# A transformer layer on one core: six lead-in tiles transposed by DMA, V in whole matmuls, and W1, W2 and Wo read from DRAM blocks

## The chip, the core and the metric

The kernel runs on one core of a Trainium2 chip. It has a matrix engine (PE, or TensorE), whose weight loads the profile lists apart as PEld; a vector engine (DVE); a scalar engine (ACT), which does the exponentials; a small general engine (POOL); and SP, which here issues every DMA. The engines run on their own and wait for each other through semaphores. The metric is the device time of one execution in microseconds; lower is better. A figure of a profile comes from one profiled execution.

## What is computed

One pre-norm transformer layer on 2048 tokens of width 1024, with 32 heads of 32 columns, a full softmax, and a feed-forward part of width 3584 with GELU:

```python
qkv = layernorm(x) @ wqkv                      # 2048 x 3072
p = softmax(q @ k.T * 32 ** -0.5)              # for each head
h = x + (p @ v) @ wo
out = h + gelu(layernorm(h) @ w1 + b1) @ w2 + b2
```

Inputs and output are bfloat16.

## The kernel before

The program is written as a list of tasks. Each task has an engine, an estimated cost, the buffers it reads and writes, and a priority. `Graph.schedule` plays the list through with these estimates and fixes the order of every engine's instructions; `assign` then works out the semaphore waits, and `emit` writes each engine's stream. Each engine does its stream strictly in order. On PE `pick_pe` chooses among the tasks that are ready: scores first (`qk`), then the products of probabilities with V (`pv`) with their row sums (`den`) when enough rounds wait, then the rest (`bg`: projections, Wo, FFN), the earliest in the list first. `merge_tiles` turns long runs of narrow matmuls (four of 32 columns side by side, L546) into whole ones of 128 columns (L549). Whole ones that were asked for as such are at L552, or at L549 after merging.

*Attention.* The 32 heads go in 8 groups of four (128 columns), and the queries in 8 blocks of 256. A job is one query block and one head group. It has 8 rounds, each over 256 keys: `Att.qk` makes the scores of four heads in four PSUM banks (L784), and two exponentials of 1024 columns (L795) write a probability tile (PT, or PX where the tile lies over memory that is used for something else later). `Job.pv` multiplies with V (L821), VectorE adds pairs of probability columns (L836), and `Job.den` sums them on PE (L850). `Job.finish` divides (L866 to L881). PSUM banks 6 and 7 are the only ones for everything else: an accumulating job holds one until it ends, and each background matmul group takes one until it is copied out.

*Lead-in.* For 16 tiles of 128 tokens the kernel loads x (`x_tile`), normalizes it (`layer_norm`, result in `xb`), and transposes it on PE (`tr_tile`: eight transposes into a bank, L619, and one copy out by ACT for tiles 0 to 3 or VectorE for the rest, L628) into `xnT`, which has four chunks of 512 tokens. After every pair of tiles comes half a chunk of keys for head group 0 (`proj_half`, L758), and three jobs (`NLJ`) start on the keys that are there: 24 rounds, whose probabilities wait in 24 tiles. V of head group 0 is made by `proj_v1` in four parts of four tiles, narrow matmuls, copied at L740. The PV of the lead may start when the last of these copies, `gate`, is done (`ready_rounds`), and the pair sums of the lead after `hold`, the last copy of keys. Then `rest_of_projections(g)` makes, for one head group after another, Q of the first 512 tokens, four chunks of keys (`proj`, L669) and V (`proj_v1` for group 1, `proj_v` from group 2, L721). The Q of tokens 512 to 1023 of some groups (`EXTRA` and group 0) goes through a staging buffer of two (`stg`) and a DRAM scratch (`qd`). Three chunks of xnT are put into DRAM scratch too (`xd`), for the Q projections of later query blocks (`late_q`), which run beside the FFN. The weights of the next head groups are loaded (`rest_w`) when the last tile of x has come.

*FFN.* For each block u of 256 tokens: `wo(u)` (its weights in four blocks of 256 columns), `ln2(u)` (layer norm, with the transposes of its two tiles by DMA, L941), `ffn1(u)` (14 blocks of W1 of 256 columns; VectorE adds the bias, and the GELU is built from a Tanh and VectorE steps), and `ffn2(u, j)` (two halves, each of 7 blocks of W2). These run beside the attention of later query blocks. The weights don't stay on chip: every u loads them again, through rings of four W1 slots (which Wo and the late Q use too) and seven W2 slots. All come straight from the inputs, so that one partition's row of a load lies in DRAM in runs of 512 bytes (Wo and W1: 256 columns) or 1024 bytes (W2: 512 columns).

*DMA.* There is one queue, SP's, and it issues in the order that the schedule fixed; an issue that has to wait holds those behind it.

Of the kernel before, what the change touches and what calls it, by code (L numbers as in the profile page):

```python
# [328 lines left out]
def build_kernel(nc, A_x, A_wqkv, A_wo, B_w1, B_b1, B_w2, B_b2, out):  # L329
# [154 lines left out]
    R1 = Rings((ffn, 4), (ffn, 7), ffn, 2)  # L484
    lq, B_lq = sb(xq_lo, "lq", [P, 2, 512], BF, 2)
# [15 lines left out]
    B_xd = [gr.buf() for _ in range(3)]  # L501
    B_qd = [[gr.buf() for _ in range(NCH)] for _ in range(G)]
# [35 lines left out]

    def mm(bank, lhsT, rhs, start, stop, reads, narrow, cols=(0, 512), after=()):

# [221 lines left out]
    class Att:  # L762
# [8 lines left out]
        def qk(self, job, r, s=None):  # L771


            qb, g = job
# [111 lines left out]
    def attention_round(job, r, lag=1):  # L886
        s = att.qk((job.qb, job.g), r)
        pending.append((job, r, s))
        attention_drain(lag)
# [7 lines left out]
    def wblock(R, src_ap, prio=1):  # L897
        s = R.next("w1", R.nw1)
        dma(R.w1[:, s, :, :], src_ap.rearrange("(dc p) c -> p dc c", p=P), P * DC * 512, writes=[R.B_w1[s]], prio=prio)
        return s  # L900

    def wo(u, tail=False):
# [3 lines left out]
        ws = [wblock(R, A_wo[:, 256 * k:256 * k + 256]) for k in range(4)]  # L906
        assert ws == [0, 1, 2, 3]
        for t in range(2):
# [3 lines left out]
            for j in range(2):  # L912
                s = ws[2 * j]
# [73 lines left out]
    def ffn2(u, j, wide=False, W=None, banks=None):  # L987
# [39 lines left out]
    LEAD_ACT = (0, 1, 2, 3)  # L1027
    NLJ = 3
    last_x = []

    def lead_norm(hc):
# [14 lines left out]
    lead_rounds = []  # L1046
    lead_norm(0)
    for hc in range(8):
# [3 lines left out]
        proj_half(1, hc, slot(), ev)  # L1052
        if hc < 7:
            lead_norm(hc + 1)
        for k, r in [(k, hc) for k in range(min(hc, NLJ))] + ([(hc, r) for r in range(hc + 1)] if hc < NLJ else []):
            n = 8 * k + r
            s = NR + 15 if n == 0 else n - 1 if n < 9 else n
            lead_rounds.append((k, r, att.qk((k, 0), r, s)))
    att.rounds = 8
    hold = [t for t in gr.tasks if t.eng == E.DVE][-1:]  # L1060
    for c in range(4):
        proj_v1(4 * c, 0, 4, slot(), "dve", 0, True)
    gate = gr.tasks[-1]
    for k in range(NLJ):
        job = Job(k, 0, slot(2))
        for _, r, s in [x for x in lead_rounds if x[0] == k]:
            job.pv(r, s)
    pool_banks = {6: [t for t in gr.tasks if t.kind == "warm"][-1:], 7: []}
    lx = last_x[-1:]

    def rest_w(blk, c0, c1):
        load_w(blk, -3, c0, c1, after=lx)
# [3 lines left out]
    rest_w(WV, P, 4 * P)  # L1076
    rest_w(WK, 2 * P, 3 * P)
# [36 lines left out]
    EXTRA = [1, 2]  # L1114
    for g in range(1, G):
# [41 lines left out]
    def ready_rounds(now):  # L1157
# [6 lines left out]
        if gate.done is None or gate.done > now + 1e-9:  # L1164
            return 0
# [112 lines left out]
```

## Time and profile before

| | |
|---|---|
| median of 3 runs | 1090.35 us (1087.95 to 1093.55) |
| the profiled execution | 1091.97 us, span 1090.2 us, mean granted PE clock 0.994 |
| HBM read, written | 161.16 MB, 10.49 MB |
| DMA queue of the kernel | 279,968 packets, 175.35 MB, 54.1% of 16 engines' span |
| instruction fetch of the largest stream | 150 packets, 2.46 MB, 0.9% |
| median issue to landing, 512 KB | W1 4.4 us, W2 5.7 us, Wo 4.2 us |

Times in a profile are microseconds from the start of the span, unless a column says ns. A group of instructions is one line, engine and operation with its tiles (out <- in, partitions x elements), its count, busy time and mean duration, and the idle time of the engine just before its members with what ended it. A wait that ends with "issue" is time in which the engine waited for nothing that the profile shows. A window gives, for a stretch, the busy time of PE, PEld, DVE, ACT and POOL with their counts, then the granted clock of PE, the mean busy share of the 16 DMA engines, and GB/s. [...]

### The profile page before, as it was taken

The page shows a single profiled execution, that of the slowest core. Times are in us where ns is not written, and L with a number is a line of the kernel's source. Part 1 is how long each engine was busy: PE and PEld are TensorE (multiplying, and loading weights), DVE is VectorE, ACT ScalarE, POOL GpSimd, SP SyncE. Part 2 cuts the span into 40 slices and gives each one's busy share as a digit, 9 for nine tenths or more (in the row PEclk, how much of TensorE's full clock was granted, in tenths as well). Part 3 has the DMA queues.
Part 4 walks back from the last instruction along what each step waited for, and adds up shares of the span by engine and source line. Part 5 has one row for each costly group of instructions (what it writes and reads, how often), then busy time and mean ns, then how long its engine had stood idle before and what let it go on. Part 6 is the DMA issues. An engine that isn't in the chain of part 4 may idle for free.

```text
span 1090.2 us, 41817 instructions
## 1 busy us (share of the span) xinstructions
PE 1045.6 (96%) x19048; PEld 609.6 (56%) x19107; DVE 755.9 (69%) x1453; ACT 1014.5 (93%) x1116; POOL 43.4 (4%) x110
## 2 busy tenths in 40 slices
PE   8989999998899999999999999999999999999998
PEld 6656555554344664574475457446545754474483
DVE  7886666666576896599489659948974967696401
ACT  4989999999999999999999999999999999999650
POOL 3200000000010001001000100100010000000100
PEclk9999999999999999999999999999999999899999
DMA  7640010008464667665685766567586656987370
GB/s 194 199 123 11 14 41 3 2 3 287 142 167 133 183 180 209 210 189 154 209 251 157 220 215 189 155 217 233 142 239 205 182 179 160 308 236 228 96 246 20
DMA packets 280146, 178.03 MB, mean 163 GB/s; under 512 B 42656, under 2 KB 274976, under 8 KB 279200
## 3 DMA queue, kind: packets, MB, share of 16 engines
q1 hardware_dynamic: 279968, 175.35, 54.1%
q8 instruction: 150, 2.46, 0.9%
q14 instruction: 28, 0.23, 0.1%
HBM read 161.16 MB, written 10.49 MB: 157 GB/s over the span
## 4 chain that ended last, share of the span: by engine, by line
PE 54%; ACT 39%; DVE 5%; issue 1%; DMA 1%; SPq 0%; POOL 0%; POOLq 0%; DVEq 0%
ACT PT L795 35%; PE ps L549 18%; PE ps L546 12%; PE ps L784 8%; PE ps L821 6%; PE ps L552 5%; PE ps L850 3%; ACT PX L795 2%; DVE PS L836 2%; ACT uu L983 2%; DMA xrb<-in_A_x_dram 0%; DVE OD L866 0%; PE ps L1025 0%; SPq L570 0%; DVE OD L873 0%
## 5 line engine op out<-in xcount | busy, mean ns | idle before, releaser
L795 ACT ACTIVATE PT<-ps 128x1024 bf16<-128x1024 f32 x992 | 922.4, 1082 | 14.7 <-PE ps L784 14.3
L836 DVE TENSOR_TENSOR PS<-PT 128x1024 bf16<-128x1024 bf16 x434 | 286.6, 685 | 128.9 <-PE ps L850 68.1
L784 PE MATMUL ps<-QT,KT 32*128 32x256 bf16 x4096 | 205.3, 274 | 10.7 <-ACT PT L795 5.4
L821 PE MATMUL ps<-PT,V 128*32 128x256 bf16 x3968 | 174.4, 274 | 2.8 <-ACT PT L795 2.8
L784 PEld LDWEIGHTS ps<-QT,KT 32*128 32x128 bf16 x4096 | 61.2, 92 | 166.3 <-ACT PT L795 134.8
L850 PE MATMUL ps<-PS,ones 128*32 128x256 bf16 x1792 | 124.6, 275 | 4.8 <-DVE PS L836 4.0
L821 PEld LDWEIGHTS ps<-PT,V 128*32 128x32 bf16 x3968 | 102.1, 97 | 29.4 <-issue 6.8
L549 PE MATMUL ps<-hnT,a_w1r 128*128 128x256 bf16 x949 | 116.5, 274 | 1.1 <-DVE gT L961 0.5
L549 PEld LDWEIGHTS ps<-hnT,a_w1r 128*128 128x128 bf16 x949 | 87.9, 98 | 25.8 <-issue 14.5
L546 PE MATMUL ps<-a_w2r,gT 128*32 128x512 bf16 x1372 | 98.3, 381 | 0.4 <-DVE hch L1007 0.2
L549 PE MATMUL ps<-a_w2r,gT 128*128 128x512 bf16 x382 | 93.8, 380 | 4.2 <-issue 2.9
L546 PE MATMUL ps<-hnT,a_w1r 128*32 128x256 bf16 x2476 | 88.9, 274 | 4.0 <-issue 1.6
L961 DVE TENSOR_TENSOR gT<-ps,b1f 128x512 bf16<-128x512 f32 x98 | 67.2, 686 | 17.5 <-PE ps L546 9.3
L546 PEld LDWEIGHTS ps<-hnT,a_w1r 128*32 128x32 bf16 x2476 | 60.4, 96 | 20.6 <-issue 16.8
L1007 DVE SCALAR_TENSOR_TENSOR hch<-ps,hch 128x512 bf16<-128x512 f32 x32 | 21.9, 685 | 69.9 <-PE ps L552 47.1
L850 PEld LDWEIGHTS ps<-PS,ones 128*32 128x32 bf16 x1792 | 47.0, 96 | 30.7 <-DVE PS L836 14.2
L549 PEld LDWEIGHTS ps<-a_w2r,gT 128*128 128x128 bf16 x413 | 35.2, 98 | 47.4 <-issue 13.4
L549 PE MATMUL ps<-xnT,Wall 128*128 128x512 bf16 (+1 forms) x256 | 53.5, 344 | 4.5 <-DVE rr L876 2.8
L983 ACT ACTIVATE uu<-uu 128x1024 bf16<-128x1024 bf16 x49 | 53.9, 1108 | 0.0
L546 PEld LDWEIGHTS ps<-a_w2r,gT 128*32 128x32 bf16 x1372 | 30.0, 96 | 25.6 <-issue 14.0
L603 POOL CAST mvb<-mv 128x2 bf16<-128x2 f32 (+1 forms) x25 | 4.9, 201 | 987.2 <-DVE mv L600 987.2
L549 PE MATMUL ps<-Wall,xnT 128*128 128x128 bf16 (+1 forms) x443 | 43.9, 247 | 0.0
(89 smaller groups left out, 1007.9 us busy)
## 6 DMA issues: line engine op xcount, KB each, us to landing
a_w2r<-in_B_w_dram SPq DMA_DIRECT2D x105, 512.0 KB, 5.7
a_w1r<-in_B_w_dram SPq DMA_DIRECT2D x98, 512.0 KB, 4.4
a_w1r<-in_A_wo_dram SPq DMA_DIRECT2D x32, 512.0 KB, 4.2
b_w1r<-in_B_w_dram SPq DMA_DIRECT2D x14, 512.0 KB, 6.1
a_w1r<-in_A_wqkv_dram SPq DMA_DIRECT2D x11, 512.0 KB, 5.0
Wall<-in_A_wqkv_dram SPq DMA_DIRECT2D x17, 256.0 KB, 4.7
xrb<-in_A_x_dram SPq DMA_DIRECT2D x16, 256.0 KB, 4.0
hch<-in_A_x_dram SPq DMA_DIRECT2D x16, 256.0 KB, 5.2
```

What stands on the lines that cost most here:

```text
L546: fns.append(lambda p, j=j: p.matmul(psum[32 * j:32 * j + 32, bi(bank), c0:c1], lhsT[:, 32 * j:32 * j + 32], rhs, start=start, stop=stop, ...
L549: t.whole = lambda p: p.matmul(psum[:, bi(bank), c0:c1], lhsT, rhs, start=start, stop=stop, skip_group_check=True)
L552: t = pe(lambda p: p.matmul(psum[:, bi(bank), c0:c1], lhsT, rhs, start=start, stop=stop), occ, reads=reads, writes=[bb(bank)], mode="full" ...
L603: pool(lambda g: g.tensor_copy(mvb[:, sl, :], mv_l[:, sl, :]), 0.25, reads=B_mv[sl], writes=B_mvb[sl], prio=prio)
L784: return p.matmul(psum[:, 2 * us[h // 2] + h % 2, 256 * i:256 * i + 256], KT[32 * h:32 * h + 32, g, k0:k0 + P], QT[32 * h:32 * h + 32, qs, :],
L795: act(lambda a, u=u, k=k: a.activation(PTs[s][:, k, :, :], psum[:, 2 * u:2 * u + 2, :], ACT.Exp, bias=0.0, scale=SCALE), 1024, reads=[B_ps ...
L821: fns.append(lambda p, i=i, h=h: p.matmul(psum[32 * h:32 * h + 32, bi(bank), 0:256], V[:, g, 2 * r + i, 32 * h:32 * h + 32], PTs[s][:, h / ...
L836: dve(lambda v: v.tensor_tensor(PS[:, n, :, :], pairs[:, :, 0:256], pairs[:, :, 256:512], ALU.add), c_dve(1024, 2), reads=B_PTs[s], writes ...
L850: fns.append(lambda p, h=h, rhs=rhs, i=i: p.matmul(psum[32 * h:32 * h + 32, bi(bank), 256:512], ones32[:, :], rhs, start=False, stop=last, ...
L961: t = dve(lambda v: v.tensor_tensor(g[:, fc:fc + 2, :], psum[:, bi(bank), :].rearrange("p (f c) -> p f c", f=2), b1f[:, fc:fc + 2].unsquee ...
L983: act(lambda a: a.activation(w, w, ACT.Tanh, bias=0.0, scale=KT2), 1024, reads=[B_uu[i]], writes=[B_uu[i]], prio=-1)
L1007: drop(dve(lambda v, hs=hs, bank=bank, half=half: v.scalar_tensor_tensor(hch[:, hs, c], psum[:, bi(bank), :], half, hch[:, hs, c], ALU.mul ...
```

## The change

In the lead-in:

- Tiles 10 to 15 are not transposed on PE. A DMA transpose of each normalized tile writes xnT (`LEAD_PE = 10`).
- `proj_v1` is asked for as whole matmuls for head groups 0 and 1.
- `gate` becomes two tasks, the last copy of keys and the last copy of V of the lead, and through `late` every matmul group that the list names after the keys of group 1 waits for both.
- A Q projection that goes through the staging buffer starts only when the buffer is free (`free`).
- The first three `rest_w` loads (group 1's keys and queries, and the rest of V's first block) wait for tile 11 of x instead of tile 15; the others wait for the last DMA transpose. The scratch copies of xnT are issued between them.

For the weights:

- `block_copies` copies Wo (2 blocks of 1 MB), W1 (14 of 512 KB) and W2 (14 of 512 KB) from the inputs into DRAM blocks by 30 DMAs from DRAM to DRAM, in which one partition's row is one run of 4 KB (W1, W2) or 8 KB (Wo). Copy i waits for exponential 96 + 5i.
- All loads of these weights then read the blocks. Wo comes as two tiles of 512 columns (`wov`), each over two W1 slots, instead of four of 256.

```diff
+    wov = [nc.alloc_sbuf_tensor_at("wov%d" % j, [P, DC, 512], BF, offset=R1.B_w1[2 * j].lo) for j in range(2)]
+    w1d = nc.dram_tensor("w1_blocks", [FC // 2, P, DC, 256], BF, kind="Internal").ap()
+    w2d = nc.dram_tensor("w2_blocks", [2, FC // 4, P, 4, 512], BF, kind="Internal").ap()
+    wod = nc.dram_tensor("wo_blocks", [2, P, DC, 512], BF, kind="Internal").ap()
...
     def mm(bank, lhsT, rhs, start, stop, reads, narrow, cols=(0, 512), after=()):
+        after = list(after) + (late if start else [])
...
+        o = B_stg[cnt["sg"] % NSG]
+        free = o.w + o.r if which == 0 and not direct else []
         for dc in range(DC):
             mm(bank, Wall[blk][:, dc, c:c + P], xnT[:, tc, dc, :], dc == 0, dc == DC - 1,
-               [B_W[blk][c // P]] + B_xnTt[tc], True)
+               [B_W[blk][c // P]] + B_xnTt[tc], True, after=free if dc == 0 else ())
...
+    def block_copies():
+
+        jobs = []
+        for j in range(2):
+            jobs.append((wod[j], A_wo[:, 512 * j:512 * j + 512].rearrange("(dc p) c -> p dc c", p=P), P * DC * 1024, B_wod[j]))
+        for k in range(FC // 2):
+            jobs.append((w1d[k], B_w1[:, 256 * k:256 * k + 256].rearrange("(dc p) c -> p dc c", p=P), P * DC * 512, B_w1d[k]))
+        for j in range(2):
+            for q in range(FC // 4):
+                jobs.append((w2d[j, q], B_w2[512 * q:512 * q + 512, 512 * j:512 * j + 512].rearrange("(f p) c -> p f c", p=P),
+                             P * 4096, B_w2d[j][q]))
+        exps = [t for t in gr.tasks if t.kind == "exp"]
+        for i, (o_ap, i_ap, n, b) in enumerate(jobs):
+            dma(o_ap, i_ap, n, writes=[b], prio=3, after=[exps[COPY0 + COPY_STEP * i]])
...
-        ws = [wblock(R, A_wo[:, 256 * k:256 * k + 256]) for k in range(4)]
-        assert ws == [0, 1, 2, 3]
+        for j in range(2):
+            dma(wov[j][:, :, :], wod[j], P * DC * 1024, reads=[B_wod[j]], writes=R.B_w1[2 * j:2 * j + 2], prio=1)
+        R.cnt["w1"] += 4
...
-                    mm(bank, OT[:, u % 3, g, t * P:(t + 1) * P], R.w1[:, s:s + 2, g, :], k == 0, k == 7 and not tail,
+                    mm(bank, OT[:, u % 3, g, t * P:(t + 1) * P], wov[j][:, g, :], k == 0, k == 7 and not tail,
...
-            s = wblock(R, B_w1[:, 256 * blk:256 * blk + 256])
+            s = wblock(R, None, block=blk)
...
-            dma(W.w2[:, s, :, :], B_w2[512 * q:512 * q + 512, c].rearrange("(f p) c -> p f c", p=P),
-                P * 4096, writes=[W.B_w2[s]], prio=1)
+            dma(W.w2[:, s, :, :], w2d[j, q], P * 4096, reads=[B_w2d[j][q]], writes=[W.B_w2[s]], prio=1)
...
+    LEAD_PE = 10
...
-            tr_tile(tt, slot(), "act" if tt in LEAD_ACT else "dve")
+            if tt < LEAD_PE:
+                tr_tile(tt, slot(), "act" if tt in LEAD_ACT else "dve")
+            else:
+                tc, t4 = divmod(tt, 4)
+                last_t[:] = [dma_transpose(xnT[:, tc, :, t4 * P:(t4 + 1) * P], xb[:, tt % NXB, :], P * 2048, [B_xb[tt % NXB]], [B_xnTt[tc][t4]], -4)]
...
-        if hc in (3, 5, 7):
-            tc = hc // 2
-            dma(xd[tc - 1], xnT[:, tc, :, :], P * 8192, reads=B_xnTt[tc], writes=[B_xd[tc - 1]], prio=1)
...
+        lead_k = gr.tasks[-1]
...
-        proj_v1(4 * c, 0, 4, slot(), "dve", 0, True)
-    gate = gr.tasks[-1]
+        proj_v1(4 * c, 0, 4, slot(), "dve")
+    gate = [lead_k, gr.tasks[-1]]
...
-    lx = last_x[-1:]
+    lx = last_x[3:4]
...
     rest_w(WV, P, 4 * P)
+    lx = last_t or last_x[-1:]
+    for tc in range(1, 4):
+        dma(xd[tc - 1], xnT[:, tc, :, :], P * 8192, reads=B_xnTt[tc], writes=[B_xd[tc - 1]], prio=1)
...
             proj(1, g, tc, slot(), "dve")
+        late[:] = gate
         if g == 1:
             for c in range(4):
-                proj_v1(4 * c, 1, 4, slot(), "dve", 0, True, [gate])
+                proj_v1(4 * c, 1, 4, slot(), "dve")
...
+    COPY0, COPY_STEP = 96, 5
...
+    block_copies()
     late_q(1, 1, [g for g in range(2, G) if g not in EXTRA])
```

More of the change, by code (lines that the diff above doesn't have):

```diff
@@ L501, in build_kernel @@
     B_xd = [gr.buf() for _ in range(3)]
+    w1d = nc.dram_tensor("w1_blocks", [FC // 2, P, DC, 256], BF, kind="Internal").ap()
+    w2d = nc.dram_tensor("w2_blocks", [2, FC // 4, P, 4, 512], BF, kind="Internal").ap()
+    wod = nc.dram_tensor("wo_blocks", [2, P, DC, 512], BF, kind="Internal").ap()
+    B_w1d = [gr.buf() for _ in range(FC // 2)]
+    B_w2d = [[gr.buf() for _ in range(FC // 4)] for _ in range(2)]
+    B_wod = [gr.buf() for _ in range(2)]
     B_qd = [[gr.buf() for _ in range(NCH)] for _ in range(G)]
@@ L537, in drop @@
             t.rel = bank
+    late = []
     def mm(bank, lhsT, rhs, start, stop, reads, narrow, cols=(0, 512), after=()):
+        after = list(after) + (late if start else [])
         c0, c1 = cols
@@ L771, in qk @@
         def qk(self, job, r, s=None):
-            qb, g = job
+            qb, g = job.qb, job.g
             qs = q_slots[qb, g]
@@ L886, in attention_round @@
     def attention_round(job, r, lag=1):
-        s = att.qk((job.qb, job.g), r)
+        s = att.qk(job, r)
         pending.append((job, r, s))
@@ L894, in attention_drain, with wblock @@
             job.pv(r, s)
-    def wblock(R, src_ap, prio=1):
+    def block_copies():
[11 more added lines that the diff above has]
+            dma(o_ap, i_ap, n, writes=[b], prio=3, after=[exps[COPY0 + COPY_STEP * i]])
+    def wblock(R, src_ap, prio=1, block=None):
         s = R.next("w1", R.nw1)
+        if block is not None:
+            dma(R.w1[:, s, :, :], w1d[block], P * DC * 512, reads=[B_w1d[block]], writes=[R.B_w1[s]], prio=prio)
+            return s
         dma(R.w1[:, s, :, :], src_ap.rearrange("(dc p) c -> p dc c", p=P), P * DC * 512, writes=[R.B_w1[s]], prio=prio)
@@ L1163, in ready_rounds @@
         waiting = 0
-        if gate.done is None or gate.done > now + 1e-9:
+        if any(x.done is None or x.done > now + 1e-9 for x in gate):
             return 0
```

11 lines of the change are left out of this document (6 added, 5 removed).

## The prediction

> **What bounds the kernel now.** I read the shares of the page first, then what ScalarE waited for, then the stages where it waited.
>
> ```profile
> span 1090.2 us, 41817 instructions
> PE 1045.6 (96%) x19048; PEld 609.6 (56%) x19107; DVE 755.9 (69%) x1453; ACT 1014.5 (93%) x1116; POOL 43.4 (4%) x110
> ACT PT L795 <- PE ps L784: 14.3, 12, 3.8
> 100.00:250.00 150.00, 148.32 (x2944) 87.08 (x2946) 95.65 (x176) 150.00 (x165) 0.00 (x0) 1.00 0.04 12
> 300.00:1000.00 700.00, 679.83 (x13007) 392.26 (x13039) 532.91 (x1023) 693.97 (x754) 22.23 (x56) 1.00 0.67 197
> 1000.00:1020.00 20.00, 18.68 (x373) 9.06 (x372) 9.30 (x17) 20.00 (x23) 0.00 (x0) 1.00 0.62 203
> 1060.00:1075.00 15.00, 14.89 (x83) 8.00 (x83) 0.73 (x2) 2.26 (x5) 0.00 (x0) 1.00 0.03 9
> ```
>
> The windows give start and end, length, then busy time of PE, PEld, DVE, ACT and POOL, granted clock, DMA share and GB/s. ScalarE is busy 150 of 150 us and 693.97 of 700: the exponentials are one unbroken line from 22.91 us to about 1020, and PE (148.32 and 679.83) runs just below it. After 1020 PE alone works, at 14.89 of 15 us, on work the change leaves alone. So time can be won where ScalarE stands still between its third exponential and the last, 14.3 us in twelve waits, and one of these (2.99 us, at 22.91) lies ahead of everything that changes. Here are the others that matter:
>
> ```profile
> 22.91 3.77 ACT L795 ACTIVATE PT<-ps 128x1024 bf16<-128x1024 f32 x4 [2.99 <-PE ps L784]
> 76.51 197.17 ACT L795 ACTIVATE PT<-ps 128x1024 bf16<-128x1024 f32 x214 [3.80 <-PE ps L784]
> 276.83 15.01 ACT L795 ACTIVATE PT<-ps 128x1024 bf16<-128x1024 f32 x16 [1.03 <-PE ps L784]
> ACT PT L795 <- PE ps L784: 8.4, 5, 3.8
> ACT PT L795 <- PE ps L784: 5.8, 7, 1.5
> ```
>
> The last two rows are the same wait within 22 to 300 us (8.4) and within 300 to 1020 (5.8). Taking off 2.99 and 3.80, 1.6 us is left, 1.03 of it at 276.83. Three terms, then: 3.8 in the lead-in, 1.6 at the start of the FFN, 5.8 under the weight traffic.
>
> **The lead-in.** One exponential takes 197.17 / 214 = 0.921 us. The lead has 24 rounds, 48 exponentials; the third starts at 22.91, so they end at 22.91 + 46 x 0.921 = 65.3. Head group 1 follows: rounds 0 to 3 read its first two key chunks (8 exponentials, to 72.7), round 4 the third chunk. ScalarE stops at 76.51 - 3.80 = 72.7 exactly. The third chunk was late:
>
> ```profile
> 55.37 0.68 DVE L740 CAST V<-ps 128x512 bf16<-128x512 f32 x1
> 61.29 0.68 DVE L669 CAST KT<-ps 128x512 bf16<-128x512 f32 x1
> 63.70 6.67 DVE L836 TENSOR_TENSOR PS<-PX 128x1024 bf16<-128x1024 bf16 x11
> 72.09 0.44 DVE L866 STREAM_TRANSPOSE OD<-ps 128x256 f32<-128x256 f32 x1
> 73.13 3.00 PE L549 MATMUL ps<-xnT,Wall 128*128 128x512 bf16 x13 [2.19 <-DVE rr L876]
> 75.11 0.65 DVE L669 CAST KT<-ps 128x512 bf16<-128x512 f32 x1
> ```
>
> Chunk two was copied at 61.29; then the lead's PV jobs held both background PSUM banks while VectorE worked off 11 pair sums, until 72.09, and chunks three and four were multiplied at 73.13. VectorE is the resource: the change takes six of its copies and 48 transposes out ahead of this.
>
> ```profile
> L628 DVE COPY xnT<-ps 128x1024 bf16<-128x1024 bf16 x6 | 4.1, 690 | 1.2 <-PE ps L619 1.1
> L619 PE MATMUL ps<-ident,xb 128*128 128x128 bf16 x48 | 3.7, 219 | 0.2 <-DVE KT L758 0.2
> hnT<-a_xb SPq DMA_TRANSPOSE x14, 3.7
> 313.11 1.24 SPq L575 DMA_TRANSPOSE hnT<-a_xb  x1
> 35.53 0.99 DVE L613 TENSOR_SCALAR xb<-xrb,mvr,rden 128x1024 bf16<-128x1024 bf16 x2
> 48.59 0.99 DVE L613 TENSOR_SCALAR xb<-xrb,mvr,rden 128x1024 bf16<-128x1024 bf16 x2
> 53.09 0.42 DVE L758 CAST KT<-ps 128x256 bf16<-128x256 f32 x1 [1.57 <-PE ps L549]
> ```
>
> So 4.1 us of VectorE and 3.7 of PE's modelled time leave the stretch from 36 to 54 us. In their place stand six DMA transposes: 1.24 us of SP's queue each (7.4 together) and 3.7 from issue to landing. Tiles 10 and 11 are normalized by 36.5 (35.53 + 0.99) and would land near 36.5 + 1.2 + 3.7 = 41.4; their half chunk of keys, the sixth, is wanted after 15 rounds, at 22.91 + 28 x 0.921 = 48.7. The last pair is normalized by 49.6, earlier if VectorE gains; it lands near 54.5 at worst, its keys are ready some 2 us later (eight matmuls and a copy of 0.42), and they are wanted at 22.91 + 40 x 0.921 = 59.8. The cover is about 3 us. SP issues head group 2's weights behind the transposes and the scratch copies of xnT later than before, but neither is read in this stretch. The weights of head group 1 now wait for tile 11 instead of tile 15, so its three later key chunks can be multiplied while the PE has no transposes to do, before PV takes the banks. One chunk ahead of the banks is enough: chunk four is wanted at 22.91 + 58 x 0.921 = 76.3, and the banks came free at 73.13. I take the whole wait, -3.8; bounds 0 (banks still held) and -4.5 (PE ahead as well).
>
> V as whole matmuls and the new waits cost nothing that I can see:
>
> ```profile
> 78.04 1.57 PE L549 MATMUL ps<-Wall,xnT 128*128 128x128 bf16 x25
> 83.59 1.52 PE L546 MATMUL ps<-Wall,xnT 128*32 128x128 bf16 x96
> ```
>
> 25 whole matmuls take 1.57 us, 96 narrow ones (24 whole) 1.52, the same; most of V already ran whole. If whole ones break up narrow runs, a 0.2 us turn on PE comes some eight times: bound +1.6, hidden as long as PE is ahead. The wait on the staging buffer sits only on three Q projections; it frees a bank instead of holding it: 0, bounds -0.5 to +0.5.
>
> **The copies.** Thirty DRAM copies start behind exponentials 96, 101 to 241: by 0.921 us, near 76.5 + 40 x 0.921 = 113 us to 247. There the DMA share is 0.04. They move 16.8 MB each way. No row shows a DRAM-to-DRAM copy; the nearest is a load in 512 B runs (next fence, 286 GB/s): 0.5 MB in 1.8 us, every 4.6 us, a share of 0.4, or 0.8 if reading and writing add up. On SP they are issued behind ScalarE's count, so a load of queries queued behind one can wait up to 4.6 us; these go out a job (16 exponentials, 14.7 us) ahead. What is exposed is PE's instruction supply, below. I take +0.6, bounds 0 and +3.
>
> **The weights in long runs.** These rows show what run length does to a full DMA: 8 KB runs (xq), 512 B (W1), 1 KB (W2).
>
> ```profile
> 262.00:264.00 2.00, 2.00 (x48) 0.92 (x48) 1.27 (x4) 2.00 (x3) 0.00 (x0) 1.00 1.02 431
> 744.50:745.50 1.00, 1.00 (x40) 0.63 (x28) 1.00 (x3) 1.00 (x2) 0.00 (x0) 1.00 0.99 286
> 808.00:811.00 3.00, 3.00 (x37) 1.10 (x39) 0.00 (x0) 3.00 (x5) 0.00 (x0) 1.00 0.93 302
> q8 instruction: 150, 2.46, 0.9%
> 815.54 0.28 PE L784 MATMUL ps<-QT,KT 32*128 32x256 bf16 x3
> 817.32 0.39 PE L784 MATMUL ps<-QT,KT 32*128 32x256 bf16 x5 [1.49 <-issue]
> PE ps L784 <- issue: 2.7, 2, 1.5
> PE ps L549 <- issue: 0.6, 4, 0.2
> ```
>
> At full share that is 423, 289 and 325 GB/s. 4 KB lies between; I take 400, nearer the long run. The share in 300 to 1000 then falls from 0.67 to about 0.67 x 300 / 400 = 0.50. No wait on a weight stands among ScalarE's, so this alone is worth nothing. But look at 815.54: eight score matmuls, one task behind one wait, are cut after the third, and PE stands for 1.49 us waiting for nothing. Its instructions were not there: 150 refills of 16.4 KB, one per 254 of PE's 38,155 instructions, go through the same DMA engines. Between 300 and 1020 us two such gaps cost 2.7 us (second to last row); between 100 and 250, with an idle DMA, the longest is 0.2 (last row). So I put most of the 5.8 us down to refills that queue behind weights. Share down by a quarter, and each burst (seven W2 blocks, 3.7 MB) shorter by 11.3 - 9.2 = 2.1 us: I take -3.3; bounds -5.8 and, by the third rival, +4. [...]
>
> **Start of the FFN.** PE has little to do until xq and the first weights land, its granted clock drops to 0.79, and the 1.03 us wait follows:
>
> ```profile
> 265.00:270.00 5.00, 3.07 (x72) 1.35 (x72) 2.60 (x5) 5.00 (x7) 0.00 (x0) 1.00 0.98 337
> 270.00:275.00 5.00, 3.47 (x46) 1.25 (x48) 2.08 (x3) 4.81 (x7) 0.00 (x0) 0.79 0.62 214
> 290.26 0.43 SPq L570 DMA_DIRECT2D a_w1r<-in_A_wo_dram  x1
> 295.52 1.68 PE L549 MATMUL ps<-a_w1r,OT 128*128 128x512 bf16 x7
> ```
>
> DMA is full there (0.98), so faster W2 helps: -0.8 of the 1.6 us. Against it Wo now comes as two 1 MB blocks that each need two ring slots free; in the trace its last block is issued at 290.26 and used at 295.52, and 0.5 MB more at 423 GB/s adds 1.2 us to that. Later passes have other PE work: +0.4, bounds 0 and +2.
>
> **The sum.** -3.8 + 0.6 - 3.3 - 0.8 + 0.4 = -6.9 us. The profiled execution took 1091.97 us (span 1090.2 and 1.8 around it), so its like would be 1085.1; it lies 1.6 above the median 1090.35, and against that the forecast is 1083.5.
>
> **Rivals.** First, slower: the DMA transposes are late and hold the gate. Every PV of the lead now waits for the last keys as well as for V. If a transpose under the lead's loads lands as late as the 1 MB xq load, 7.0 us,
>
> ```profile
> xq<-x_scratch SPq DMA_DIRECT2D x3, 1024.0 KB, 7.0
> ```
>
> and queues behind one other, the last pair lands at 49.6 + 2.4 + 7.0 = 59.0 and the gate opens near 61 instead of 56.1 (55.37 + 0.68): ScalarE first dries up at 59.8 for 1.2 us, and the 3.8 us wait grows by 4.9. That is +6.1, time 1096.5 with no gain elsewhere. It decides once landing takes over 3 us more than 3.7. For it: 0.95 to 0.98 DMA share occurs when weights load; against it: by 50 us the x tiles are all in.
>
> Second, the lead's wait stays, since only the PSUM banks matter and PV is still picked before the third chunk: 1083.5 + 3.8 = 1087.3. For it: banks were what PE waited for at 73.13; against: 7.8 us of work left both engines just before.
>
> [...]
>
> **Chances.** Forecast 0.53, own range 1079 to 1087; transposes late 0.14; lead wait stays 0.17; refills later 0.16. A change of 0.5% is 5.5 us, about what can be told from none here (the three runs spread over 5.6 us). Below 1084.9 I put most of the forecast and a little of the second: 0.5. Above 1095.8: most of the first and the tail of the third: 0.15. The rest, 0.35, is within. The range, with the bounds of the terms and the third rival inside: 1078 to 1093.
>
> **What would show it.** ScalarE's wait near 72 gone, KT's third chunk copied before 72; if it is there, the lead step is wrong. No PE gap over 1 us without a releaser after 300 and ScalarE's sum of waits there near 2.5 us; 5 or more and the refill step is wrong. DMA share near 0.5 in 300 to 1000. A share near 0.4 from 110 to 245 with ScalarE still unbroken. PE late at wo near 295 shows the Wo price. The whole fails if ScalarE gains the 3.8 early and PE, busy 148.32 of 150 us behind it, gives it back before 260.

## The result, and the profile after

The changed kernel takes 1086.88 us (median of 7 runs, 1085.57 to 1088.87) against 1091.46 us before (7 runs, 1087.95 to 1093.6): a ratio of 0.9951, 95% interval 0.9934 to 0.9968. That is 0.49% faster, clear of no change and right at the 0.5% bound. The forecast was 1083.5 us, range 1078 to 1093: right side, 3.4 us too hopeful. The profiled execution took 1087.09 us (forecast for it: 1085.1; before 1091.97).

The page's first lines, the sum of ScalarE's waits, and the two long stretches (start and end, length, busy time of PE, PEld, DVE, ACT, POOL, clock, DMA share, GB/s):

```profile
span 1085.3 us, 41670 instructions
PE 1045.5 (96%) x18957; PEld 608.6 (56%) x19014; DVE 755.3 (70%) x1447; ACT 1014.5 (93%) x1116; POOL 43.2 (4%) x110
ACT PT L807 <- PE ps L796: 10.5, 16, 3.0
100.00:250.00 150.00, 148.32 (x2881) 86.15 (x2888) 95.32 (x174) 149.94 (x165) 0.00 (x0) 1.00 0.41 125
300.00:1000.00 700.00, 682.14 (x13117) 394.92 (x13141) 535.63 (x1024) 695.89 (x757) 22.08 (x56) 1.00 0.59 199
```

ScalarE's waits on scores fell from 14.3 to 10.5 us. From 100 to 250 the DMA went from a share of 0.04 to 0.41 and ScalarE stayed unbroken (149.94 of 150). From 300 to 1000 the share fell from 0.67 to 0.59, not to 0.50, and ScalarE gained 1.9 us. ScalarE's timeline shows what waits are left; the last column is the idle time ahead and what ended it:

```profile
21.91 3.77 ACT L807 ACTIVATE PT<-ps 128x1024 bf16<-128x1024 f32 x4 [3.00 <-PE ps L796]
72.40 1.94 ACT L807 ACTIVATE PT<-ps 128x1024 bf16<-128x1024 f32 x2 [0.83 <-PE ps L796]
82.90 12.99 ACT L807 ACTIVATE PT<-ps 128x1024 bf16<-128x1024 f32 x14 [0.71 <-PE ps L833]
295.63 11.12 ACT L807 ACTIVATE PT<-ps 128x1024 bf16<-128x1024 f32 x12 [1.12 <-PE ps L796]
460.76 2.85 ACT L807 ACTIVATE PT<-ps 128x1024 bf16<-128x1024 f32 x3 [0.46 <-PE ps L796]
937.64 8.36 ACT L807 ACTIVATE PT<-ps 128x1024 bf16<-128x1024 f32 x9 [0.72 <-PE ps L796]
973.99 4.71 ACT L807 ACTIVATE PT<-ps 128x1024 bf16<-128x1024 f32 x5 [1.27 <-PE ps L796]
```

The wait of 3.80 us that ended at 76.51 has become 0.83 at 72.40 with smaller ones after it, 2.3 us between 30 and 110. New are 1.12 at 295.63 and, from 0.35 to 0.72, the one at 937.64. The first exponentials start 1.0 us earlier (21.91 against 22.91); they do so in every later kernel too (21.6 to 22.5, and 22.27 with the old lead-in), so that part of the difference is not put down to the change. VectorE in the lead-in of after:

```profile
46.51 0.69 DVE L681 CAST KT<-ps 128x512 bf16<-128x512 f32 x1 [1.17 <-PE ps L559]
48.68 0.69 DVE L681 CAST KT<-ps 128x512 bf16<-128x512 f32 x1 [0.56 <-PE ps L559]
55.51 0.42 DVE L770 CAST KT<-ps 128x256 bf16<-128x256 f32 x1 [3.24 <-PE ps L559]
57.78 0.69 DVE L752 CAST V<-ps 128x512 bf16<-128x512 f32 x1
58.88 0.69 DVE L681 CAST KT<-ps 128x512 bf16<-128x512 f32 x1 [0.41 <-PE ps L556]
```

Group 1's third key chunk is copied at 48.68 instead of 75.11 and the fourth at 58.88: both in hand before ScalarE wants them. But VectorE stands idle for 3.24 us ahead of the last keys, and the gate opens at 58.5 (57.78 + 0.69) instead of 56.1. The last DMA transpose is issued at 49.0 and lands 3.1 us later; PE multiplies the last keys from 53.09 on, and stands 0.85 us for ScalarE in between.

The kernels are in one table. Ratios are to before, timed on the same chip; waits are ScalarE's on PE, in us, from one profiled execution each. That execution is not always a typical one: against its kernel's median it took 4.0 us less in e1, 3.3 less in e6, 2.0 less in e10 and 2.3 more in e2 (0.2 more in after, the same in e3). e5 is the kernel of e9 (ratio 1.0034); its profiled execution took 2164.7 us against 1093 to 1099 in the nine others, and is left out here with its cause open.

| kernel | ratio, 95% interval | 30-110 | 110-255 | 255-310 | 310-1020 | of these 285-305, 930-950 |
|---|---|---|---|---|---|---|
| before | 1 | 3.8 | 0 | 1.6 | 5.8 | 0.4, 0.4 |
| after | 0.9951 [0.9934, 0.9968] | 2.3 | 0 | 2.1 | 3.9 | 1.1, 0.7 |
| e1 weights only | 0.9965 [0.9947, 0.9983] | 5.6 | 0 | 1.4 | 2.2 | 1.2, 1.5 |
| e2 lead only | 0.9976 [0.9960, 0.9992] | 2.2 | 0 | 1.5 | 9.4 | 0, 0.4 |
| e3 short runs | 0.9977 [0.9964, 0.9990] | 2.3 | 0 | 2.1 | 7.7 | 1.1, 0.9 |
| e4 PE transposes | 0.9959 [0.9943, 0.9974] | 4.7 | 0.2 | 2.9 | 2.6 | 1.3, 1.0 |
| e6 Wo in four | 0.9914 [0.9882, 0.9946] | 1.1 | 0 | 1.2 | 1.4 | 0, 0 |
| e7 narrow V | 0.9980 [0.9962, 0.9998] | 4.1 | 0 | 2.7 | 7.1 | 1.3, 0.8 |
| e8 PE to tile 11 | 0.9951 [0.9936, 0.9967] | 1.6 | 0 | 2.4 | 7.1 | 2.3, 1.8 |
| e9 copies in bursts | 1.0027 [1.0006, 1.0048] | 2.2 | 4.9 | 2.6 | 6.2 | 1.3, 1.8 |
| e10 shift 128 | 0.9932 [0.9904, 0.9960] | 2.3 | 0.2 | 2.0 | 2.0 | 1.0, 1.4 |
| e11 shift 64 | 0.9914 [0.9885, 0.9944] | 2.2 | 0 | 1.5 | 4.1 | 1.3, 1.7 |
| e12 Wo in four, shift 128 | 0.9922 [0.9890, 0.9953] | 2.3 | 0 | 1.1 | 3.5 | 0, 0 |

### The profile page after: what moved, and what is told of

It is laid out like the page before. It is cut to its first block, busy times and chain, and to the rows that moved or that the text cites. A ratio compares the mean times of both kernels' runs of the same rounds, so it can differ in the third digit from the quotient of the medians.

```text
span 1085.3 us, 41670 instructions
## 1 busy us (share of the span) xinstructions
PE 1045.5 (96%) x18957; PEld 608.6 (56%) x19014; DVE 755.3 (70%) x1447; ACT 1014.5 (93%) x1116; POOL 43.2 (4%) x110
## 4 chain that ended last, share of the span: by engine, by line
ACT 65%; PE 30%; DVE 3%; issue 1%; POOL 0%; POOLq 0%; DVEq 0%
ACT PT L807 60%; PE ps L559 8%; PE ps L562 6%; PE ps L556 6%; PE ps L796 4%; ACT uu L1014 3%; PE ps L833 3%; ACT PX L807 2%; PE ps L862 2%; DVE PS L848 1%; PE ps L1055 1%; PE ps L629 0%; DVE uu L1013 0%; ACT xnT L636 0%; DVE hch L1037 0%
## 5 line engine op out<-in xcount | busy, mean ns | idle before, releaser
L807 ACT ACTIVATE PT<-ps 128x1024 bf16<-128x1024 f32 x992 | 924.5, 1085 | 11.4 <-PE ps L796 10.5
L833 PE MATMUL ps<-PT,V 128*32 128x256 bf16 x3968 | 176.8, 274 | 3.4 <-ACT PT L807 3.2
L862 PE MATMUL ps<-PS,ones 128*32 128x256 bf16 x1792 | 127.1, 276 | 3.5 <-DVE PS L848 2.5
L559 PE MATMUL ps<-hnT,a_w1r 128*128 128x256 bf16 x979 | 119.1, 273 | 1.9 <-DVE hch L1037 1.1
L559 PEld LDWEIGHTS ps<-hnT,a_w1r 128*128 128x128 bf16 x979 | 90.1, 98 | 27.0 <-issue 15.9
L556 PE MATMUL ps<-a_w2r,gT 128*32 128x512 bf16 x1380 | 100.8, 381 | 0.6 <-DVE gT L1016 0.4
L559 PE MATMUL ps<-a_w2r,gT 128*128 128x512 bf16 x390 | 96.2, 380 | 2.8 <-issue 1.9
L556 PE MATMUL ps<-hnT,a_w1r 128*32 128x256 bf16 x2356 | 84.3, 275 | 3.3 <-issue 1.8
L878 DVE STREAM_TRANSPOSE OD<-ps 128x256 f32<-128x256 f32 x64 | 28.5, 446 | 13.7 <-PE ps L862 6.7
```

The lines of the kernel that those rows point to most:

```text
L556: fns.append(lambda p, j=j: p.matmul(psum[32 * j:32 * j + 32, bi(bank), c0:c1], lhsT[:, 32 * j:32 * j + 32], rhs, start=start, stop=stop, ...
L559: t.whole = lambda p: p.matmul(psum[:, bi(bank), c0:c1], lhsT, rhs, start=start, stop=stop, skip_group_check=True)
L807: act(lambda a, u=u, k=k: a.activation(PTs[s][:, k, :, :], psum[:, 2 * u:2 * u + 2, :], ACT.Exp, bias=0.0, scale=SCALE), 1024, reads=[B_ps ...
L833: fns.append(lambda p, i=i, h=h: p.matmul(psum[32 * h:32 * h + 32, bi(bank), 0:256], V[:, g, 2 * r + i, 32 * h:32 * h + 32], PTs[s][:, h / ...
L862: fns.append(lambda p, h=h, rhs=rhs, i=i: p.matmul(psum[32 * h:32 * h + 32, bi(bank), 256:512], ones32[:, :], rhs, start=False, stop=last, ...
L878: t = dve(lambda v: v.transpose(OD[:, o, 1, :], psum[:, bi(bank), 256:512]), 0.36, reads=[self.B_O, self.B_D], writes=B_D, prio=-1)
```

## The experiments

**The two halves, and run length by itself.** e1 is before with the copies, DRAM blocks and their readers (from `wov` to `block_copies()`) and nothing of the lead-in; e2 is after without these. e3 keeps everything of after, and the order on PE, VectorE, ScalarE and GpSimd, but lays the blocks out so that a load still comes in runs of 512 B and 1 KB:

```diff
-    w1d = nc.dram_tensor("w1_blocks", [FC // 2, P, DC, 256], BF, kind="Internal").ap()
+    w1d = nc.dram_tensor("w1_blocks", [FC // 2, DC, P, 256], BF, kind="Internal").ap().rearrange("k d p c -> k p d c")
...
```

and w2d and wod in the same way.

> The copies and long-run weights alone, on the lead-in of before. If instruction refills queue behind the weights: ScalarE's waits between 300 and 1020 us fall from 5.8 to 4 or less, no gap of PE over 1.2 us without a releaser there, time 2 us (1 to 3) under before, ratio 0.998. If the weights' transfers are hidden anyway and the gaps do not depend on them: those waits stay at 5 to 6.5 and the time within 1 us of before. In both cases the 3.8 us wait near 72 us stays, and DMA share in 300 to 1000 falls to 0.59.

> The lead-in of the changed kernel alone, weights read in short runs from the inputs, no copies. If the gain is the sum of two independent parts: ScalarE's lead wait falls from 3.8 to about 2.3 with the rest, its waits in 300 to 1020 stay near 5.8, time 2.5 us under before (1.5 to 3.5), ratio 0.9977. If long runs do nothing, it gives all of the 4.6 us, ratio 0.995, with waits in 300 to 1020 of 4 or less. If the late gate of the DMA transposes is paid behind the lead, less than 1 us is gained.

> The changed kernel with the same copies and the same order on PE, VectorE, ScalarE and GpSimd, but the DRAM blocks laid out so that each load still comes in runs of 512 B (W1) and 1 KB (W2, Wo). If run length is what shortens the FFN's waits: DMA share in 300 to 1000 back near 0.67, ScalarE's waits in 300 to 1020 from 3.9 to 5 or more, time 2 us over the changed kernel (1 to 3.5), ratio to before 0.997. If it was the other order of instructions: share 0.67 but waits 3.9 and ratio 0.995.

Sums of ScalarE's waits from 310 to 1020, first e1, then e3 and e2 (total, number, longest), and the DMA of e3 from 300 to 1000:

```profile
ACT PT L802 <- PE ps L791: 2.2, 4, 1.5
```

```profile
ACT PT L807 <- PE ps L796: 7.7, 12, 1.3
300.00:1000.00 700.00, 682.89 (x13059) 392.34 (x13048) 534.43 (x1021) 692.07 (x751) 22.06 (x56) 1.00 0.65 197
```

```profile
ACT PT L800 <- PE ps L789: 9.4, 14, 2.1
```

e3 is the cleanest pair: the same instructions in the same order as after, only the run length differs. The waits go from 3.9 to 7.7 us in the profile; the ratio goes from 0.9951 to 0.9977, 2.8 us, but the intervals still overlap by 0.0004. One profile each is not enough, since e9 below, with the PE program of after, has 6.2 us there. The kernels together say the same as the pair: the three that load W1 and W2 in short runs (before, e2, e3) wait 5.8 to 9.4 us, 7.6 on average, the ten with long runs 1.4 to 7.1, 4.0 on average. So the runs point to run length, and not to blocks, copies or order by themselves. e1 gains 0.0035 by the weights alone, 3.8 us, and its waits have the smaller size; e2 gains 0.0024, 2.6 us, by the lead-in alone, though its waits here came out at 9.4 and not near 5.8 as expected. Added up (0.9941) the halves agree with after within the intervals. The old lead-in's wait stayed in e1, at 5.4 instead of 3.8 us: 14 matmuls of group 1's keys took 4.79 us there, 0.34 each, against 3.00 for 13, with a granted clock of 0.71 from 70 to 75.

**What the lead-in owes to which edit.** e4 and e8 change `LEAD_PE = 10` to 16 and 12; e7 asks for narrow V again:

```diff
-        proj_v1(4 * c, 0, 4, slot(), "dve")
+        proj_v1(4 * c, 0, 4, slot(), "dve", 0, True)
...
-                proj_v1(4 * c, 1, 4, slot(), "dve")
+                proj_v1(4 * c, 1, 4, slot(), "dve", 0, True)
```

> The changed kernel with all 16 tiles transposed on PE again (earlier weights, whole V, the order of PV kept). If the DMA transposes are what frees VectorE for the third key chunk: its copy comes after 72 us again, the lead wait goes back to 3 us or more, time 2 us over the changed kernel, ratio to before 0.997. If they only hold the gate back and the earlier weights bring the chunk forward: VectorE has no idle stretch of 2 us at 50 to 56 us, the last K copy is at 54 or before, the lead waits are 1 us or less, and the time is 0.5 to 1.5 us under the changed kernel, ratio 0.994.

> The changed kernel with tiles 10 and 11 transposed on PE again, so that four instead of six DMA transposes stand before the last keys. If the queue of six holds the gate back (58.5 us against 56.1 before) and that is what is left of the lead's waits: last K copy at 54.5 or before, the fourth key chunk of head group 1 still copied before 72, lead waits 1.5 us or less, time 0.5 to 1 us under the changed kernel. If the gate does not matter: lead waits stay near 2.3, or rise to 4.7 as with all 16 on PE when the fourth chunk misses its place ahead of PV.

> The changed kernel with the V projections of head groups 0 and 1 as narrow matmuls again, as before the change. If whole matmuls for V are worth nothing, as the prediction has it: lead waits between 60 and 110 us within 0.7 us of 2.3, time within 1 us of the changed kernel. If whole V is a part of the gain (fewer, longer matmuls in front of PV): lead waits 3 us or more, time 1 us over it. If it costs (turns between narrow and whole): lead waits 1.5 or less.

With all tiles on PE (e4), two rows of VectorE and one of ScalarE:

```profile
63.83 0.64 DVE L681 CAST KT<-ps 128x512 bf16<-128x512 f32 x1
77.32 0.69 DVE L681 CAST KT<-ps 128x512 bf16<-128x512 f32 x1 [1.10 <-PE ps L559]
78.67 5.61 ACT L807 ACTIVATE PT<-ps 128x1024 bf16<-128x1024 f32 x6 [3.27 <-PE ps L796]
```

The earlier weights alone bring the third chunk to 63.83, in time, and the stall moves one chunk on: the fourth is copied at 77.32 and ScalarE stands 3.27 us for it. Only with the DMA transposes do both chunks pass ahead of the PV jobs. The time differs by 0.0008, less than this can tell, though the lead waits went from 2.3 to 4.7.

With four DMA transposes (e8) the last keys are copied at 55.29 instead of 55.51 and the gate opens at 58.25: the length of the queue is not what sets them. The waits behind the lead fall to 0.8, but a new one of 0.83 appears at 54.33, and the ratio is that of after. In e6 below, with the lead-in of after, the waits at 72.40 and 74.59 (0.83 and 0.26) are gone; PE is as busy from 60 to 80 (18.12 of 20 us in both), the gate opens no earlier, and the clock is 1.00 instead of 0.91. In e12, with the work of e6, the clock is 0.91 again and a wait of 0.94 is back at 73.04. So these 1.1 us of after go with a lowered clock and not with the late gate. All later kernels but e6 have 0.91 there, before has 1.00; what lowers it was not tried.

Narrow V (e7), which the prediction prices at nothing, has lead waits of 4.1 and a ratio of 0.9980. The cut is in the middle of a den group, rows of PE and of DMA in e7, then the same stretch in after:

```profile
76.10 0.39 PE L862 MATMUL ps<-PX,ones 128*32 128x256 bf16 x6
77.95 0.29 PE L862 MATMUL ps<-PX,ones 128*32 128x256 bf16 x2 [1.47 <-issue]
76.00:78.00 2.00, 0.53 (x18) 0.25 (x18) 1.83 (x4) 1.90 (x3) 0.00 (x0) 1.00 1.25 278
```

```profile
76.00:78.00 2.00, 2.00 (x50) 1.25 (x42) 2.00 (x4) 1.95 (x3) 0.00 (x0) 1.00 1.23 280
```

Eight matmuls behind one wait stop after six, for 1.47 us, while the loads of the next groups' weights fill the DMA (1.25; the kernel's own queue alone takes the share past 1, with 1.20 of after's 1.23). It has the form of before's gap at 817.32. From 60 to 80 PE runs 527 matmuls instead of 424: narrow V costs no PE time (in before 1.52 us for 96 matmuls, against 1.57 for 25 whole ones) but four times the instructions, and the refills that bring them (149 of 16.4 KB in after) meet a DMA at a share of 1.25 here. How much of the 3.2 us in the ratio is narrow V stays open: 1.8 us more lie in the lead, but 3.2 more lie in 310 to 1020, where V has no part, and the intervals of e7 and after overlap.

**Refills in the open.** If a full DMA starves PE of instructions, it must do so where no weights are waited for. e5 and e9, the same kernel, issue the thirty copies seven at a time:

```diff
-            dma(o_ap, i_ap, n, writes=[b], prio=3, after=[exps[COPY0 + COPY_STEP * i]])
+            dma(o_ap, i_ap, n, writes=[b], prio=3, after=[exps[COPY0 + 7 * COPY_STEP * (i // 7)]])
```

> The changed kernel with the same thirty DRAM copies in the same stretch (110 to 250 us), issued seven at a time every 35 exponentials instead of one every five; PE, VectorE, ScalarE and GpSimd have the same order, and no instruction of PE or ScalarE in that stretch needs a copied block. If it is PE's instruction refills that a full DMA makes late: with bursts of some 12 us at full share, gaps of PE over 0.5 us without a releaser appear there (before and after: none over 0.33), ScalarE waits 1 to 4 us in 100 to 250 instead of 0.1, and the time is 1 to 4 us over the changed kernel. If the gaps in the FFN come from something else in it (weights, order): 100 to 250 stays unbroken, ScalarE 149.9 of 150, time as the changed kernel.

> The kernel with the copies in bursts of seven once more, since the execution profiled first took 2164.7 us against 1093 to 1099 in the nine others. From these nine the bursts cost about 9 us against the changed kernel. If refills queued behind the bursts are the cause: ScalarE's waits on PE between 100 and 255 us add up to 5 us or more, right behind gaps of PE without a releaser in stretches of DMA share 0.9 or more, and nothing waits for a load of queries by over 1 us in sum. If late query loads behind the bursts are the cause: the waits stand behind PE or ScalarE waiting for QT from the DMA.

Stretches of e9, the rows of PE with the longest gaps, and ScalarE's waits:

```profile
150.00:160.00 10.00, 8.89 (x235) 6.09 (x228) 5.38 (x11) 9.06 (x11) 0.00 (x0) 1.00 0.97 270
160.00:170.00 10.00, 9.95 (x168) 6.17 (x171) 6.10 (x12) 9.98 (x11) 0.00 (x0) 1.00 0.01 2
180.00:190.00 10.00, 10.00 (x269) 7.17 (x267) 5.82 (x11) 10.00 (x12) 0.00 (x0) 1.00 1.03 307
190.00:200.00 10.00, 8.18 (x93) 4.22 (x90) 4.18 (x10) 8.27 (x10) 0.00 (x0) 1.00 0.38 117
157.83 0.40 PE L833 MATMUL ps<-PT,V 128*32 128x256 bf16 x8 [1.11 <-issue]
192.92 0.71 PE L559 MATMUL ps<-Wall,xnT 128*128 128x256 bf16 x5 [1.77 <-issue]
158.94 33.35 ACT L807 ACTIVATE PT<-ps 128x1024 bf16<-128x1024 f32 x36 [0.94 <-PE ps L796]
194.01 27.83 ACT L807 ACTIVATE PT<-ps 128x1024 bf16<-128x1024 f32 x30 [1.72 <-PE ps L796]
ACT PT L807 <- PE ps L796: 4.9, 4, 1.7
```

The stretch that ran unbroken under spread copies now has four waits, 4.9 us, each at the end of a burst, and nothing on PE waits for a DMA there. The time is 1.0027 of before (1.0034 in e5), 8 to 9 us over after, where 1 to 4 were expected, and the gain is a loss. The bursts show 4.9 us of it; 2.3 more are waits in 310 to 1020, where nothing but the point in time differs. In the trace's records of the queue "q8 instruction", the 16 KB refills, a refill begins shortly ahead of the end of each gap:

```
kernel   refill begins   PE resumes   between
before        431.87       434.30       2.43
before        814.87       817.32       2.45
after         969.97       972.45       2.48
e9            126.22       128.61       2.39
e9            155.63       157.83       2.20
e9            190.51       192.92       2.41
e9            219.63       221.80       2.17
```

The refill takes 0.9 to 1.0 us; PE resumes 2.2 to 2.5 us after it starts in all seven. In the thirteen traces of the table PE has 50 gaps of over 0.4 us without a releaser between 60 and 1018 us. 48 of them end 2.2 to 2.6 us after a refill began, and the other two 3.1 and 3.2 us after, behind refills that took 1.9. Refills come some 7 us apart (6.8 on average in before and in after, from 60 to 1018 us), so chance does not do that: together with the bursts it settles the cause of these gaps. At a DMA share of 0.41 after has no gap over 0.2 us from 100 to 250; e9 has one of 1.77 us once the same copies come in bursts.

e10 and e11 leave the DMA alone and move PE's instructions against it: 64 or 32 of the 80 warm-up matmuls are split in two of half the columns, so that all later instructions stand 128 or 64 further on.

```diff
-        pe(lambda p: p.matmul(psum[:, 6, 0:256], ident[:, :], b2t[:, 0:256], start=True, stop=True), 0.18 if k < 42 else 0.115,
+        fns = [lambda p, c=c: p.matmul(psum[:, 6, c:c + 128], ident[:, :], b2t[:, c:c + 128], start=True, stop=True) for c in (0, 128)]
+        if k >= 64:
+            fns = [lambda p: p.matmul(psum[:, 6, 0:256], ident[:, :], b2t[:, 0:256], start=True, stop=True)]
+        pe(fns, 0.18 if k < 42 else 0.115,
```

> The changed kernel with 64 of its 80 warm-up matmuls each split in two of half the columns: the same order on every engine behind them, but all later instructions of PE stand 128 further on, half a refill. If the waits in 310 to 1020 are refills that fall into stretches of full DMA: they move, at most two of the five of 0.3 us and more (433.6, 460.8, 747.7, 937.6 and 974.0) stay, and the sum changes from 3.9 by 1 us or more in one of the two shifts. If they belong to the work at these places (weights, banks, order): at least four of the five stay and the sum is 3.9 within 1 us.

> The same with 32 warm-up matmuls split, a shift of 64 instructions, a quarter of a refill. Expected as for 128; by the refill theory the places differ from those of both other phases, and times of the three phases may differ by up to 4 us (the sums seen so far with long runs are 1.4 to 7.1).

ScalarE's waits from 310 to 1020 and the longest one, e10 and then e11:

```profile
ACT PT L807 <- PE ps L796: 2.0, 3, 1.4
937.33 8.35 ACT L807 ACTIVATE PT<-ps 128x1024 bf16<-128x1024 f32 x9 [1.39 <-PE ps L796]
```

```profile
ACT PT L807 <- PE ps L796: 4.1, 5, 2.0
934.93 3.77 ACT L807 ACTIVATE PT<-ps 128x1024 bf16<-128x1024 f32 x4 [1.50 <-PE ps L796]
972.66 4.71 ACT L807 ACTIVATE PT<-ps 128x1024 bf16<-128x1024 f32 x5 [2.02 <-PE ps L796]
```

The work is the same, and the waits of after near 434 and 461 are gone in both; the one near 974 is gone in e10 and 2.02 in e11. Only the wait near 937 stays in both; no gap without a releaser stands ahead of it, so it has another cause. In e9, whose PE program is that of after, three waits of after come back at the same work 5 to 8 us later, at 466.30, 754.10 and 982.39. So the places go with how refills fall against full stretches of DMA. The sum without the wait near 937 is 0.6 (e10), 2.4 (e11) and 3.2 us (after), but 4.4 in e9 at the position of after, and 6.3 in e7: with one profile each, what the position does to the sum can't be told from what differs between executions. The ratios, 0.9932 and 0.9914, are below that of after, but the intervals overlap.

**Wo.** e6 reads Wo from the input in four 512 KB blocks again, with the rest of after; the two copies of Wo are still made and nothing reads them. e12 adds the shift of 128.

```diff
-        for j in range(2):
-            dma(wov[j][:, :, :], wod[j], P * DC * 1024, reads=[B_wod[j]], writes=R.B_w1[2 * j:2 * j + 2], prio=1)
-        R.cnt["w1"] += 4
+        ws = [wblock(R, A_wo[:, 256 * k:256 * k + 256]) for k in range(4)]
+        assert ws == [0, 1, 2, 3]
```

> The changed kernel with Wo read straight from the input in four 512 KB blocks of 256 columns again (the two copies of Wo are still made and not read). If the two 1 MB blocks are what brings ScalarE's wait of 1.1 us near 295 us (with the clock at 0.66 there): no wait of over 0.5 us between 285 and 300, waits in 255 to 310 fall from 2.1 to 1.5 or less, time 0.5 to 1 us under the changed kernel. If it comes from PE running out of work there: a wait of 1 us or more stays near 295, time within 0.5 us.

> The kernel with Wo in four blocks from the input, PE shifted by 128 instructions as above. It was at 0.9914 of before, with waits of 1.1 in the lead, 1.2 in 255 to 310 and 1.4 in 310 to 1020, against 2.3, 2.1 and 3.9 of the changed kernel. If the four blocks of Wo are what gains: ratio 0.990 to 0.993 again, no wait near 295, waits in 310 to 1020 of 2.5 or less. If its gain in the FFN was the place of the refills: waits there rise to 3.5 or more, ratio 0.993 to 0.995, and only the 0.9 us near 295 is left of it.

PE's first matmuls of wo and the window around them, after and then e6:

```profile
292.76 2.49 PE L559 MATMUL ps<-wov,OT 128*128 128x512 bf16 x6 [0.33 <-issue]
290.00:295.00 5.00, 3.23 (x22) 1.11 (x23) 3.10 (x8) 4.51 (x5) 0.00 (x0) 0.66 0.34 115
```

```profile
291.28 1.68 PE L558 MATMUL ps<-a_w1r,OT 128*128 128x512 bf16 x7
290.00:295.00 5.00, 4.05 (x38) 1.56 (x38) 3.11 (x6) 5.00 (x6) 0.00 (x0) 1.00 0.34 104
```

The table's last column has no exception: the nine kernels that read Wo in 1 MB blocks have 1.0 to 2.3 us of waits near 295 and 0.7 to 1.8 near 937; the four that read 512 KB blocks (before, e2, e6, e12) have 0.4 at most. But these four pay earlier, all ahead of the same exponential: 1.03 us at 276.83 in before, 1.14 in e2, 0.95 in e6 and 1.06 in e12. Of the nine, three have nothing around there (e1, e8, e11). The row of e6, and what after has in its place:

```profile
273.13 27.85 ACT L806 ACTIVATE PT<-ps 128x1024 bf16<-128x1024 f32 x30 [0.95 <-PE ps L795]
272.14 22.37 ACT L807 ACTIVATE PT<-ps 128x1024 bf16<-128x1024 f32 x24 [0.39 <-PE ps L796]
```

So the fair measure is all of 255 to 310: 1.4 to 2.9 us with 1 MB blocks, 1.1 to 1.6 without.

In after the first matmuls of wo start 0.43 us apart (2.49 us for the six recorded), in e6 0.22 us (1.68 for seven). The granted clock is 0.66 against 1.00, so the scores queue behind slow matmuls. The blocks are not late: they land at 284.2 (278.84 + 5.4) and 293.7 (284.04 + 9.7) and are used from 292.76 and 295.51 on. PE has run low on other work (3.26 busy of 5 us from 285 to 290 in after, 3.95 in e6) and its clock has been lowered when they start. The clock is 1.00 from 280 to 290 and 0.66 from 290 to 295, and the longest gap of PE from 280 to 297 is 1.44 us, the one that ends at 291.81. Why PE runs low earlier with 1 MB blocks was not tried; their size, their two slots and the order that the schedule then fixes change together.

Near 937 PE is not at Wo but at the FFN's first product (`hnT,a_w1r`), in after 44 narrow matmuls between two scores. A low clock by itself does not bring the wait there, since before and e6 have one too, with waits of 0.4 and 0. Rows of after, before and e6:

```profile
930.00:935.00 5.00, 4.18 (x60) 1.15 (x60) 1.60 (x3) 5.00 (x7) 0.00 (x0) 0.50 0.92 341
940.00:945.00 5.00, 4.68 (x56) 1.98 (x52) 2.56 (x7) 5.00 (x6) 0.00 (x0) 0.50 1.10 366
930.00:935.00 5.00, 4.19 (x56) 1.96 (x60) 2.71 (x7) 5.00 (x6) 0.00 (x0) 0.66 0.87 329
```

The cause of the wait near 937 stays open.

e6 at 0.9914 (1084.12 against 1093.59 us of before on that chip) shares the lowest ratio with e11. It beats before; against after the intervals overlap by 0.0012. e12 came out between its two expectations: the ratio, 0.9922, and no wait near 295 or 937 as if the blocks gain, but waits in 310 to 1020 up from 1.4 to 3.5 as if the places of the refills had been luck. e10 and e12 are the same pair at the other position, 0.9932 with 1 MB blocks and 0.9922 without, with 6.5 and 6.9 us of waits in all. So what the blocks of Wo cost in time is not shown.

## Why the prediction came out as it did

The sum had five terms, -6.9 in all. The profiled execution gained 4.9: 1.0 at the start, which the change does not explain, 3.0 in the waits that the terms are about, and 0.9 spread over the rest, which is not attributed.

- **Lead-in, -3.8: mechanism right, size 1.5** (3.80 to 2.27 in the profile; 2.6 us in e2's time, interval 0.9 to 4.4). The third chunk did move ahead, from 75.11 to 48.68. "VectorE is the resource" was half of it: e4, with all six copies back on VectorE, has the third chunk at 63.83, in time, by the earlier weights; the DMA transposes bring the fourth. The step that failed is "I take the whole wait": PE's work around the PV jobs was taken at full clock, and 1.1 us came with a clock of 0.91; the rest (0.71 behind a PV, 0.47 at 96.35) stands in e6 as well (0.61 and 0.47). "One chunk ahead of the banks is enough" fell too: in e4 the third chunk was early and the fourth cost 3.27.
- **V as whole matmuls, 0 with a bound of +1.6: the sign may be wrong.** It was priced by PE time, where the rows agreed (1.57 and 1.52 us). Priced by instructions, the narrow form can cost a late refill under a full DMA: e7's lead waits are 1.8 us longer, one gap of 1.47 among them. The prediction had that price for the FFN and did not apply it here. Whether the gap comes with narrow V or with where one refill fell is not shown; no other position of it was run.
- **Copies, +0.6: 0.** 149.94 of 150 us. The cover was their spacing: in bursts the same copies bring 4.9 us of waits in their own stretch, beyond the +3 of the bound.
- **Long runs, -3.3: mechanism right, and the size too for the waits that stand behind such gaps.** In before six gaps of over 0.4 us without a releaser, and not only the two among the scores, stand within 4 us ahead of 5.5 of the 5.8 us of waits; in after three, ahead of 2.2 us. The other waits there grew from 0.4 to 1.7, among them 0.72 at 937.64, so the sum fell by 1.9 (5.8 to 3.9). The pair with e3 has 3.8 us of waits, e1 3.8 us of time: single profiles differ by as much as these sizes do, so that 3.3 was met is in part luck. The row at 815.54, cut after three of eight matmuls, was read rightly. The DMA share, 0.59 instead of 0.50, was mis-sized mainly by the rate. In the trace of after from 300 to 1000 the 4 KB packets moved 104 MB in a share of 0.42, which is 354 GB/s at full share and not 400 (before: 512 B 289, 1 KB 330); that queries, x, outputs and transposes keep their runs makes up about a third of the miss. A gap of 1.11 us without a releaser, at 972.45, and 3.9 us of waits lie between what was to show the step right (2.5) and wrong (5).
- **Start of the FFN and Wo, -0.8 and +0.4: together +0.4 in 255 to 310 (1.65 to 2.06 by the single waits), and 0.4 more near 937.** Wo is the term that was mis-sized: over 255 to 310 and 930 to 950 together the nine kernels with 1 MB blocks wait 2.8 to 4.4 us, the other four 1.1 to 2.0; after 2.8 against 2.0 before: +0.8, and over the bound of +2 in e8 and e9. The route was wrong as well: near 295 not a late block but a lowered clock, and near 937 work that is not Wo's.

Of the rivals, the first (late DMA transposes) happened in part: the gate opened 2.4 us later, but the last keys came at 55.9, 2.8 us ahead of the 58.8 at which ScalarE, 1.0 us earlier here than before, wants them (21.91 + 40 x 0.921), and it cost nothing that can be shown. The second did not happen. The third, later refills with long runs, has e3 and the averages against it; no run shows the +4 us that it puts into the range: ScalarE waited 4.0 us on average from 310 to 1020 with long runs, and 7.6 with short ones. The terms missed by 3.9 us: 2.3 in the lead-in, 1.4 in the FFN, 0.8 at its start and Wo, less 0.6 for the copies. 1.1 us of it, in the lead-in, goes with PE's clock, and so does part of the wait near 295; the prediction read the clock from the windows and then left it out of every term but one.

## What to carry to other kernels

Where matmuls are short, count instructions as a load on the DMA (here 149 refills of 16.4 KB): spread background copies (no wait from 110 to 255 in after, 4.9 us in e9), prefer long runs (waits of 3.9 us in after, 7.7 in e3), and be wary of quadrupling PE's instruction count in a stretch that loads weights, because here each burst of some 10 us at full share cost a PE gap of 0.8 to 1.8 us. Before a stall is priced at zero, ask at what clock the work behind it will run: PE that had run low on background work came back at half speed (0.43 us from one matmul to the next instead of 0.22), and what waited behind it paid. Where the profile's waits move when nothing but the position of the instructions moves, judge an edit by runs and by a controlled pair at more than one position, not by one profile.

## What was not expected of the hardware

- With the same order on every engine, ScalarE's waits from 310 to 1020 were 3.9, 4.1 and 2.0 us with PE's program 0, 64 and 128 of 38,000 instructions further on, and 6.2 in e9 with it where it was but the stretch some 5 us later (one execution each).
- PE resumed 2.2 to 2.5 us after the late refill began, though the refill's own packet took 0.9 to 1.0 us.
